# A retention layer with a Strassen-Winograd MLP: transposes in TensorE's transpose mode, another queue for k, and seven products for three quarters of block 1's first layer

## The chip, the cores and the metric

The kernel runs on one core of one Trainium2 chip. A time is the device time of one execution in microseconds (us). The median of nine executions stands for the kernel; the profile shows one execution more closely. TensorE does the matrix products, ScalarE (ACT), VectorE (DVE) and GpSimd (POOL) the elementwise work, and DMAs are issued by the queues of SyncE (SP), ACT and POOL. TensorE writes to PSUM, from where ScalarE and VectorE take its results.

## What is computed

Two stages. The first is a recurrent retention over 4 batches, 8 heads, 768 positions and 64 dimensions; the second is an MLP over the 3072 tokens that come out, 512 to 2048 to 512 wide, with a sigmoid-approximated GELU between its two layers.

```python
for t in range(S):
    state = gamma[None, :, None, None] * state + np.einsum('bhd,bhe->bhde', k[:, :, t], v[:, :, t])
    y[:, :, t] = scale * np.einsum('bhd,bhde->bhe', q[:, :, t], state)
x = y.transpose(0, 2, 1, 3).reshape(B * S, H * D)
h = x @ w_in
g = h * (1.0 / (1.0 + np.exp(-1.702 * h)))
out = g @ w_out
```

All data of q, k, v and of the result are 32-bit floats. The two weight matrices arrive as 64-bit floats and are narrowed to 32 bits on the chip.

## The kernel before

**Tiling.** The 768 positions are cut into chunks of 64, and two batches are worked on at a time, so there are 24 steps of attention, each with all 8 heads of two batches. Four steps give the 512 tokens of one block, and there are six blocks m = 0 to 5. The MLP of a block has an `up` half (x times w_in, then GELU into the tiles G) and a `down` half (G times w_out). Attention steps 0 to 7, the narrowing of both weight matrices, the `up` half of block 0 (`up0`) and the `up` half of block 1 (`up1`) come first, in an order that is written out by hand in one long string of names; after it, a loop over the blocks interleaves `down` of block m with the attention of later blocks. Blocks 2 to 5 have their `up` half (`up`, line 464 ff.) as seven products in place of eight, after Strassen and Winograd; blocks 0 and 1 have it as plain products.

**Order.** TensorE follows the program order. On the other engines, an instruction passed to `pin` (or `tc.keep_in_program_order`) keeps its place among the pinned ones of its engine; the others are placed by the framework's scheduler. Each engine works through its own queue in order, and a wait at its head holds up what is behind it. A named buffer (a tag of a pool with so many `bufs`) is given to its next user only when the last reader of the one before is done.

**The first 104 us.** For a step j below 6, `load` fetches q, k and v in their natural layout, 128 KB for each of the two batches (line 138), k of step 0 by ACT's queue and all others by SP's. `turn` (lines 239 to 249) turns q and k on TensorE, by ordinary products with a unit matrix: for every pair of heads s and s + 4 one product of 64 columns for the lower and one for the upper half of the output's partitions. The compiled program has two weight loads and two matmul instructions for every 32-bit product, so a turn of q and k together has 32 instructions. `turned` copies the result out of PSUM on ACT (line 260), `decay` scales k head by head on ACT (line 271), `attend` does the products of a step (lines 288 to 311), `masked`, `by_state`, `output`, `updated` follow on VectorE, `aged` on ACT. From step 6 on, q and k are fetched in 128-byte rows (line 155), turned by VectorE (line 252), and scaled by GpSimd (lines 273 and 358).

**Narrowing.** A weight tile of 512 KB is fetched as raw 64-bit words by SP's queue (`fetch`, line 178) into one of three raw buffers that rotate; the pair of tiles of number n uses raw buffer n modulo 3, so it waits until tile n - 3 is done. `abs` on ACT (line 205) starts the conversion, `half` (lines 209 to 211) and `rest` (lines 215 to 220) on VectorE end it. Numbers 0 to 7 are w_in, 8 to 15 w_out. A product `up0.th.p` needs w_in's number p.

**Block 1's first layer.** `up1(f)`, lines 419 to 427, for the 16 tiles f of 128 hidden units: four products of 512 columns into one PSUM tile, then `gate` (line 392) from PSUM to G on ACT. The two PSUM tiles rotate. X1, the input of block 1, lies in a part of W2 and is complete with `x7`.

**Down of block 0.** The first part of `down(0)` (line 708) needs w_out's numbers 0 and 1 in its first quarter, 2 and 3 in its second, 4 and 5 in its third, 6 and 7 (narrowing numbers 14 and 15) in its fourth. VectorE's `sums_w2` and `sums_g` (lines 446 to 457) prepare the operands of the third and later parts.

Below, "T0" is the moment when TensorE ends `up0.1.7` and goes on to block 1's first layer, 104.3 us in the profile.

Of the kernel before, what the change touches and what calls it, by code (L numbers as in the profile page):

```python
# [9 lines left out]
F32 = mybir.dt.float32  # L10
U32 = mybir.dt.uint32
AF = mybir.ActivationFunctionType
# [16 lines left out]
def kernel(  # L29
# [95 lines left out]
    def load(j, what="qkv"):  # L125

        b, c = j // NC * 2, j % NC
        rows = slice(c * D, (c + 1) * D)  # L130
        keep = tc.keep_in_program_order if j < 2 * CB else lambda i: i

        def plain(name, src, tag, bufs, engine=sp):
            t = two.tile([P, H, D], F32, name=name + "_in", tag=tag, bufs=bufs)
            QKV[name, j] = t
            for i in range(2):
                if j < NEW:
                    keep(engine.dma_start(t[i * D:(i + 1) * D], src[b + i, :, rows, :].rearrange("h p d -> p h d")))
                else:
                    for r in range(2):  # L140
                        keep(engine.dma_start(t[r * D:(r + 1) * D, i * HP:(i + 1) * HP],
                                              src[b + i, r * HP:(r + 1) * HP, rows, :].rearrange("h p d -> p h d")))

        if j < NEW:
            if "q" in what:
                plain("q", q, "q_sq", 2)
            if "k" in what:
                plain("kn", k, "k_sq", 2, sp if j else act)
        elif "q" in what:
            for name, src in (("q", q), ("k", k)):  # L150
# [88 lines left out]
    def turn(j):  # L239

        QT[j], KT[j] = home(j, "qT"), home(j, "kT")
        if j < NEW:

            x = QKV.pop(("q", j)), QKV["kn", j]
            TURNED[j] = p = [ps.tile([P, HP, P], F32, name="pt", tag="y") for i in range(2)]
            for n in (1, 0) if j else (0, 1):
                for s in range(HP):
                    for r in range(2):
                        pe.matmul(p[n][HALF[r], s, :], x[n][:, HP * r + s, :], ident, start=True, stop=True)  # L249
# [12 lines left out]
    def decay(j):  # L262

        if j % NC == NC - 1:
            return
        KD[j] = home(j, "kd")
        x = QKV["kn", j]
        if j < NEW:

            for h in range(H):  # L270
                pin(act.activation(KD[j][:, h], x[:, h], AF.Copy, scale=cold[:, H + h:H + h + 1]))
        else:
            pool.tensor_mul(KD[j].rearrange("p (i s) d -> p i s d", i=2), x.rearrange("p (i s) d -> p i s d", i=2),
                            cold[:, None, H:H + HP, None].to_broadcast([P, 2, HP, D]))
# [144 lines left out]
    def up1(f):  # L419
# [6 lines left out]
            pe.matmul(h, w, X1[:, c // 2:4:2, c % 2, :], start=(c == 0), stop=(c == 3))  # L426
        return G[:, p, ab:4:2, :], h


    def sums_w1(p):  # L430
        t, q1 = w1(p)
# [358 lines left out]

    def halves_anew():

        pool.dma_start(whole_h, bass.AP(tensor=col_decay.tensor, offset=col_decay.offset + (D - 1) * W + H,
                                        ap=[[0, P], [1, H]]))
# [16 lines left out]
    for j in range(2 * CB):  # L811
        for name in "qkv":
            works[f"{name}{j}"] = lambda j=j, name=name: load(j, name)
        works |= {f"{name}{j}": lambda j=j, do=do: do(j) for name, do in (
            ("turn", turn), ("turned", turned), ("decay", decay), ("masked", masked), ("state", by_state),
            ("x", output), ("aged", aged), ("updated", updated))}
        for f in (None, *range(2 * CB)):
            works[f"step{j}" + ("" if f is None else f"-{f}")] = lambda j=j, f=f: attend(j, f)
        works[f"step-{j}"] = lambda j=j: attend(None, j)
    for i in range(2 * NFF):  # L820
        works[f"w{i // 2}{'ab'[i % 2]}"] = lambda i=i: fetch(i)
    for name, i in [("0a", 0), ("0b", 1)] + [(str(p), 2 * p) for p in range(1, NFF)]:
# [19 lines left out]

    begin()
    for name in """
        k0 table q0 warm turn0 w0b rows warm k1 abs0b q1 turned0 step0 v0 w0a half0b mask turn1 causal rest0b
        masked0 decay0 v1 decay1 abs0a half0a step-0 updated0 turned1 q2 step1 rowd k2 whole w2b turn2 w2a x0 k3
        aged1 masked1 turned2 v2 rest0a abs2 q3 step-1 updated1 state1 decay2 aged2 step2 q4 x1 half2 decay3 w3b
        w3a up0.0.0 masked2 turn3 k4 step-2 v3 q5 rest2 k5 gate0.0.0 turned3 updated2 state2 step3 up0.0.2
        masked3 abs3 half3 x2 rest3 turn4 w1b step-3 aged3 gate0.0.2 turned4 state3 w1a w5b updated3 v5 decay4
        abs1 x3 turn5 half1 up0.0.3 turned5 up0.1.2 step4 aged4 w5a rest1 v4 gate0.0.3 decay5 w6a masked4  # L850
        gate0.1.2 abs5 w6b step5-4 half5 rest5 up0.0.1 updated4 abs6 state4 gate0.0.1 w4b
# [104 lines left out]
```

## Time and profile before

| | us |
|---|---|
| median of 9 executions | 667.01 (665.6 to 669.49) |
| the profiled execution's own time | 667.08 |
| its span, first to last instruction | 665.4 |
| granted TensorE clock, mean share | 0.997 |
| TensorE busy with matmuls | 649.7 (98%) |
| VectorE, ACT, GpSimd busy | 435.4, 148.6, 175.7 |
| `up1` of block 1 (line 426), 128 matmul instructions, on the chain of waits | 54.93 |
| turns of q and k on TensorE (line 249), 192 matmul instructions, busy | 15.8 |

The profile of one execution is read through several views. The page's first parts give the busy time of each engine and its share in 40 slices. The chain of waits follows the work that ended last back from the last instruction, at each step to what released it, in order of time: start, length, and the engine, tile and line. The timeline lists instructions of an engine by start and length, with the idle time before them and what ended it. "PE" is a matmul, "PEld" a weight load, and "SPq" an issue of a DMA by SP's queue. A busy matmul engine isn't a fast one: the busy time of pipelined matmuls overlaps and hides short gaps. So the time of a run of matmuls is best taken from the chain, where it is the distance from start to start.

### The profile page before, as it was taken

Reading aid. Unit: us, or ns where it says so; the run is one execution under the profiler, and the core shown is the slowest. Engines: PE = TensorE matmul, PEld = TensorE weight load, DVE = VectorE, ACT = ScalarE, POOL = GpSimd, SP = SyncE. Lnnn points to the kernel's source line nnn. Section 1 sums busy time; section 2 is a strip of 40 time slices with the busy share of each in tenths; the row PEclk is TensorE's granted clock in tenths of the full one; section 3 lists DMA queues with packets and bytes.
Section 4 is the critical chain, followed back from the end, with each engine's and each line's share of the span. In section 5 each row is a group of like instructions: output and inputs, shape, how many; then the busy total and the mean of one; then the engine's idle time right before and its main releaser. Section 6 shows DMA issues by size and latency. Waiting matters only on the chain.

```text
span 665.4 us, 15234 instructions
## 1 busy us (share of the span) xinstructions
PE 649.7 (98%) x6438; PEld 563.8 (85%) x6438; DVE 435.4 (65%) x618; ACT 148.6 (22%) x285; POOL 175.7 (26%) x196
## 2 busy tenths in 40 slices
PE   7899999999999999999999999999999999999997
PEld 4787875446888888888999888999888999988997
DVE  3798778788545775456985345995254995254965
ACT  5673222231000000233110234010233110233110
POOL 3000310000268326100446500345700255500000
PEclk9899999999999999999999999999999999999999
DMA  9996647442203546263385742286652253602142
GB/s 189 214 227 188 169 81 232 162 91 35 46 10 135 171 106 186 63 217 133 85 221 132 243 101 95 80 194 156 193 158 96 63 150 109 229 25 95 52 157 95
DMA packets 150500, 89.49 MB, mean 135 GB/s; under 512 B 136192, under 2 KB 137472, under 8 KB 149408
## 3 DMA queue, kind: packets, MB, share of 16 engines
q1 hardware_dynamic: 140944, 46.50, 30.5%
q0 software_dynamic: 7184, 40.78, 17.0%
q10 hardware_dynamic: 2304, 1.25, 0.7%
q8 instruction: 50, 0.82, 0.5%
q14 instruction: 18, 0.15, 0.1%
HBM read 72.89 MB, written 15.47 MB: 133 GB/s over the span
## 4 chain that ended last, share of the span: by engine, by line
PE 88%; DMA 5%; DVE 3%; SPq 2%; POOL 1%; issue 1%; ACT 0%; POOLq 0%; DVEq 0%
PE pq L575 24%; PE px L471 16%; PE pd L708 13%; PE py L471 12%; PE ph L426 8%; PE ph L413 5%; PE pa L288 2%; PE pa L296 2%; PE py L305 2%; PE py L311 2%; DMA kn_in<-in_k_dram 1%; PE pt L249 1%; DMA W<-in_moe_w_out_dram 1%; DMA k_sq<-in_k_dram 1%; DMA q_in<-in_q_dram 1%
## 5 line engine op out<-in xcount | busy, mean ns | idle before, releaser
L575 PE MATMUL pq<-W,G 128*128 128x128 f32 x672 | 80.5, 276 | 0.4 <-issue 0.4
L575 PEld LDWEIGHTS pq<-W,G 128*128 128x128 f32 x672 | 77.6, 192 | 1.2 <-issue 0.6
L544 POOL DMA_DIRECT2D ring<-W2D x28 | 15.4, 551 | 228.7 <-PE px L471 118.2
L471 PE MATMUL px<-X,W1A 128*128 128x256 f32 x256 | 60.0, 380 | 0.4 <-POOL X L441 0.4
L471 PE MATMUL px<-X,W1B 128*128 128x256 f32 x256 | 59.8, 379 | 0.0
L575 PE MATMUL pq<-ring,own 128*128 128x128 f32 x448 | 59.8, 276 | 0.0
L575 PEld LDWEIGHTS pq<-ring,own 128*128 128x128 f32 x448 | 54.5, 192 | 0.4
L471 PEld LDWEIGHTS px<-X,W1A 128*128 128x128 f32 x256 | 48.2, 190 | 7.3 <-POOL X L441 1.0
L471 PEld LDWEIGHTS px<-X,W1B 128*128 128x128 f32 x256 | 48.5, 190 | 6.7
L708 PE MATMUL pd<-W,G 128*128 128x256 f32 x224 | 49.6, 381 | 0.0
L708 PEld LDWEIGHTS pd<-W,G 128*128 128x128 f32 x224 | 42.2, 190 | 5.9
L471 PE MATMUL py<-X,W1A 128*128 128x256 f32 x192 | 45.4, 379 | 0.0
L471 PE MATMUL py<-X,W1B 128*128 128x256 f32 x192 | 45.4, 379 | 0.0
L392 ACT ACTIVATE G<-G 128x512 f32<-128x512 f32 x48 | 30.2, 630 | 52.0 <-DVE G L481 33.4
L471 PEld LDWEIGHTS py<-X,W1A 128*128 128x128 f32 x192 | 36.5, 190 | 5.0
L471 PEld LDWEIGHTS py<-X,W1B 128*128 128x128 f32 x192 | 36.5, 190 | 5.0
L489 DVE TENSOR_TENSOR t<-py,u 128x512 f32<-128x512 f32 x16 | 11.1, 692 | 32.7 <-PE py L471 32.7
L478 ACT ACTIVATE p<-px 128x512 f32<-128x512 f32 x16 | 9.6, 597 | 94.6 <-PE px L471 94.6
L575 PE MATMUL pq<-ring,G 128*128 128x128 f32 x224 | 29.6, 275 | 0.0
L575 PE MATMUL pq<-W,own 128*128 128x128 f32 x224 | 29.6, 275 | 0.0
L413 PE MATMUL ph<-X,W1A 128*128 128x256 f32 x128 | 29.0, 382 | 0.2 <-DVE X L346 0.2
L503 DVE TENSOR_TENSOR G<-G 128x512 f32<-128x512 f32 (+2 forms) x24 | 12.3, 514 | 25.7 <-ACT G L392 25.7
(206 smaller groups left out, 1165.2 us busy)
## 6 DMA issues: line engine op xcount, KB each, us to landing
ring<-W2D POOLq DMA_DIRECT2D x28, 768.0 KB, 4.8
W1B<-W1D POOLq DMA_DIRECT2D x6, 1792.0 KB, 9.4
W<-in_moe_w_in_dram SPq DMA_DIRECT2D x12, 512.0 KB, 5.7
W<-in_moe_w_out_dram SPq DMA_DIRECT2D x10, 512.0 KB, 6.1
out_dram<-o POOLq DMA_DIRECT2D x20, 256.0 KB, 3.4
q_sq<-in_q_dram SPq DMA_DIRECT2D x144, 32.0 KB, 2.3
k_sq<-in_k_dram SPq DMA_DIRECT2D x144, 32.0 KB, 2.2
v_in<-in_v_dram SPq DMA_DIRECT2D x72, 64.0 KB, 2.9
```

Of the source, the lines that this page charges most:

```text
L288: pe.matmul(pa[HALF[w], u, 0, s, :], kt[HALF[u], w, s, :], qt[HALF[u], w, s, :], start=True, stop=True)
L296: pe.matmul(pa[HALF[u], w, 1, s, :], kd[HALF[w], HP * u + s, :], vn[HALF[w], HP * u + s, :], start=True, stop=True)
L305: pe.matmul(py[HALF[o], u, 1, 2 * w + s2, :], old[HALF[u], w, 2 * s2 + o, :], qt[HALF[u], w, 2 * s2 + o, :], start=True, stop=True)
L311: pe.matmul(py[HALF[o], w, 0, 2 * u + s2 if f < NEW else 2 * s2 + u, :], vn[HALF[w], HP * u + s, :], a[HALF[w], u, s, :], start=True, stop ...
L392: pin(act.activation(g, h[:, i], AF.Gelu_apprx_sigmoid))
L413: pe.matmul(h[:, ab], w, X[:, 2 * th + c // 2, c % 2, :], start=(ab == 0 and c == 0), stop=(c == 3), skip_group_check=True)
L426: pe.matmul(h, w, X1[:, c // 2:4:2, c % 2, :], start=(c == 0), stop=(c == 3))
L471: pe.matmul(acc[:, u, :], t[:, q1 + u, sa, c, :], X[:, sb, c, :], start=(start and u == 0 and c == 0), stop=(stop and c == 1), skip_group_ ...
L503: dve.tensor_sub(q[0][1], q[0][0], q[0][1])
L544: pool.dma_start(c, W2D[i])
L575: pe.matmul(p0[:, j, :], a[:, d], w[:, d], start=(new and j == 0 and d == 0), stop=(d == NP // 2 - 1), skip_group_check=True)
L708: pe.matmul(p0[:, n, :], g1(m, p, sa)[:, n * P:(n + 1) * P], W2[:, sb, p, :], start=(new and p == 0 and n == 0), stop=(last and p == NP - ...
```

## The change

1. **Turns.** For steps 0 to 5, `turn` has, for each of q and k, four transposes of 128 columns in TensorE's transpose mode in place of eight ordinary products of 64 columns. A 128-column operand must hold heads s and s + 4 side by side, so `load` puts head n * 4 + s at place 2 * s + n. For this, each fetch of q and k of 128 KB becomes two of 64 KB. `decay` reads k at the new places.
2. **Queues and buffers of k.** From step 1 on, k goes by GpSimd's queue and not SP's. The k of steps 2 and 3 goes to the buffers of the outputs ("o"), which nothing else uses at this time, and `k2` stands before `turn1` in the order. Around it, `q2`, `updated0`, `decay1`, `masked1` and `decay3` change their places. A small fetch of GpSimd's in `halves_anew` is pinned.
3. **Seven products.** Twelve of block 1's sixteen `up1` are replaced: for d = 2, 0, 1, `seven(d, k)` has seven products of two by two tiles with 256 columns, in the scheme of `up`. GpSimd makes the sums of the operands, four for x (`seven_x`) and four for each d (`seven_w`), in buffers that the attention and the outputs use at other times. ACT copies three partial results out of PSUM for each d, VectorE adds four, and ACT gates four. `up1.12` to `up1.15` stay as they are. The narrowing of w_out (numbers 11, 10, 12, 14, 13, 15) is spread anew between them.

The diff, cut to its core:

```diff
@@ load @@
                 if j < NEW:
-                    keep(engine.dma_start(t[i * D:(i + 1) * D], src[b + i, :, rows, :].rearrange("h p d -> p h d")))
+                    to, at = t[i * D:(i + 1) * D], src[b + i, :, rows, :].rearrange("h p d -> p h d")
+                    for n in range(1 if name == "v" else 2):
+                        keep(engine.dma_start(*((to, at) if name == "v" else (to[:, n:H:2], at[:, n * HP:(n + 1) * HP]))))
...
-                plain("kn", k, "k_sq", 2, sp if j else act)
+                plain("kn", k, "k_sq" if j in (0, 1, 4, 5) else "o", 2, pool if j else act)
@@ turn @@
                 for s in range(HP):
-                    for r in range(2):
-                        pe.matmul(p[n][HALF[r], s, :], x[n][:, HP * r + s, :], ident, start=True, stop=True)
+                    pe.matmul(p[n][:, s, :], x[n][:, 2 * s:2 * s + 2].rearrange("p r d -> p (r d)"), ident, is_transpose=True)
@@ decay @@
-                pin(act.activation(KD[j][:, h], x[:, h], AF.Copy, scale=cold[:, H + h:H + h + 1]))
+                pin(act.activation(KD[j][:, h], x[:, h % HP * 2 + h // HP], AF.Copy, scale=cold[:, H + h:H + h + 1]))
@@ new, beside up1 @@
+    def seven_x():
+        for n, (tag, bufs) in ((4, ("q_sq", 2)), (5, ("k_sq", 2)), (6, ("kn", 1)), (2, ("tmp", 1))):
+            SUM_X[n] = two.tile([P, 2, TH], F32, name=f"x{n}", tag=tag, bufs=bufs)
+        for to, a, b in ((SUM_X[4], X1[:, 2], X1[:, 0]), (SUM_X[5], X1[:, 3], SUM_X[4]),
+                         (SUM_X[6], X1[:, 3], X1[:, 2]), (SUM_X[2], X1[:, 1], SUM_X[5])):
+            pin(pool.tensor_sub(to, a, b))
+    def seven_w(d):
...
+        pin(pool.tensor_add(m[4], w[2], w[3]))
+        pin(pool.tensor_sub(m[5], m[4], w[0]))
+        pin(pool.tensor_sub(m[6], w[0], w[2]))
+        pin(pool.tensor_sub(m[2], w[1], m[5]))
+    def seven(d, k):
...
+        acc = SEVEN[f"y{k}" if k in (1, 3, 5) else "x"]
+        product(acc, (0, 1, 5, 4, 6, 2, 3)[k], (0, 1, 5, 4, 6, 3, 2)[k], k in (0, 1, 3, 5), k in (1, 3, 5, 6))
+        if k == 0:
+            kept("p1", "s1", acc)
+        elif k == 1:
+            pin(dve.tensor_add(a[0], acc, SEVEN["p1"]))
+            hidden(a[0], a[0])
+        elif k == 2:
+            kept("u", "s2", acc)
+        elif k == 3:
...
+            pin(dve.tensor_add(SEVEN["t"], acc, SEVEN["u"]))
+        elif k == 4:
+            kept("vv", "s3", acc)
+        elif k == 5:
+            pin(dve.tensor_add(a[3], SEVEN["y3"], SEVEN["vv"]))
+            hidden(a[3], a[3])
+            pin(dve.tensor_add(a[2], acc, SEVEN["t"]))
+            hidden(a[2], a[2])
+        else:
+            hidden(a[1], acc)
@@ the order @@
-        k0 table q0 warm turn0 w0b rows warm k1 abs0b q1 turned0 step0 v0 w0a half0b mask turn1 causal rest0b
-        masked0 decay0 v1 decay1 abs0a half0a step-0 updated0 turned1 q2 step1 rowd k2 whole w2b turn2 w2a x0 k3
-        aged1 masked1 turned2 v2 rest0a abs2 q3 step-1 updated1 state1 decay2 aged2 step2 q4 x1 half2 decay3 w3b
-        w3a up0.0.0 masked2 turn3 k4 step-2 v3 q5 rest2 k5 gate0.0.0 turned3 updated2 state2 step3 up0.0.2
+        k0 table q0 warm turn0 w0b rows warm k1 abs0b q1 turned0 step0 v0 w0a half0b mask k2 turn1 causal rest0b
+        masked0 decay0 q2 v1 step-0 updated0 turned1 decay1 step1 rowd masked1 abs0a half0a whole w2b turn2 w2a x0 k3
+        aged1 turned2 v2 rest0a abs2 q3 step-1 updated1 state1 decay2 aged2 step2 q4 x1 half2 w3b
+        w3a up0.0.0 masked2 turn3 k4 step-2 v3 q5 rest2 k5 turned3 gate0.0.0 decay3 updated2 state2 step3 up0.0.2
...
-        w11a w11b step-7 state7 x7 half9 w10b w10a up0.1.7 rest9 gate0.1.7 abs11 half11 up1.8 gate1.8
-        w12a w12b rest11 up1.5 gate1.5 up1.4 gate1.4 abs10 half10 up1.0 gate1.0 rest10 up1.3 gate1.3 abs12
-        aged7 updated7 up1.2 gate1.2 w14b w14a half12 up1.6 gate1.6 rest12 up1.9 gate1.9 abs14 half14 w13a w13b
-        up1.11 gate1.11 rest14 up1.10 gate1.10 abs13 half13 w15a w15b up1.7 gate1.7 rest13 abs15 half15 up1.12
-        gate1.12 late_loads up1.13 gate1.13 rest15 up1.15 gate1.15 up1.14 gate1.14 up1.1 gate1.1
+        w11a w11b step-7 state7 x7 half9 w10b w10a seven_w2 up0.1.7 rest9 gate0.1.7 abs11
+        seven_x seven2.0 seven2.1 half11 seven2.2 seven2.3 w12a w12b rest11 seven2.4 seven2.5 aged7 seven_w0 abs10 seven2.6
+        seven0.0 seven0.1 half10 seven0.2 seven0.3 rest10 w14b w14a seven0.4 seven0.5 seven_w1 abs12 seven0.6
+        updated7 seven1.0 seven1.1 half12 seven1.2 seven1.3 rest12 w13a w13b seven1.4 abs14 seven1.5 half14
+        seven1.6 up1.12 rest14 gate1.12 abs13 half13 w15a w15b late_loads up1.13 gate1.13 rest13 abs15 half15
+        up1.15 gate1.15 rest15 up1.14 gate1.14
```

More of the change, by code (lines that the diff above doesn't have):

```diff
@@ L427, in up1 @@
         return G[:, p, ab:4:2, :], h
+    SUM_X, SUM_W = {}, {}
+    def seven_x():
[5 more added lines that the diff above has]
+    def seven_w(d):
+        t, q1 = w1(2 * d)
+        w = [t[:, q1:q1 + 2, s].rearrange("p u c f -> p u (c f)") for s in range(4)]
+        SUM_W[d] = {4: one.tile([P, 2, 2 * P], F32, name="w4", tag="qT", bufs=2),
+                    5: one.tile([P, 2, 2 * P], F32, name="w5", tag="at", bufs=2),
+                    6: two.tile([P, 2, 2 * P], F32, name="w6", tag="o"),
+                    2: one.tile([P, 2, 2 * P], F32, name="w2", tag="kT")}
+        m = SUM_W[d]
+        pin(pool.tensor_add(m[4], w[2], w[3]))
+        pin(pool.tensor_sub(m[5], m[4], w[0]))
+        pin(pool.tensor_sub(m[6], w[0], w[2]))
+        pin(pool.tensor_sub(m[2], w[1], m[5]))
@@ new lines, with product, kept @@
+    SEVEN = {}
+    def seven(d, k):
+        t, q1 = w1(2 * d)
+        a = [G[:, 2 * d:2 * d + 2, s, :] for s in range(4)]
+        def product(acc, sa, sb, start, stop):
+            for u in range(2):
+                for c in range(2):
+                    w = SUM_W[d][sa][:, u, c * P:(c + 1) * P] if sa in (4, 5, 6, 2) else t[:, q1 + u, sa, c, :]
+                    x = SUM_X[sb][:, c, :] if sb in SUM_X else X1[:, sb, c, :]
+                    pe.matmul(acc[:, u, :], w, x, start=(start and u == 0 and c == 0), stop=(stop and c == 1),
+                              skip_group_check=True)
+        def kept(name, tag, src):
+            SEVEN[name] = one.tile([P, 2, TH], F32, name=name, tag=tag)
+            pin(act.activation(SEVEN[name], src, AF.Copy))
+        if k in (0, 1, 3, 5):
+            SEVEN["x" if k == 0 else f"y{k}"] = ps.tile([P, 2, TH], F32, name="ph", tag="x" if k == 0 else "y")
+        acc = SEVEN[f"y{k}" if k in (1, 3, 5) else "x"]
[8 more added lines that the diff above has]
+        elif k == 3:
+            SEVEN["t"] = one.tile([P, 2, TH], F32, name="t", tag="s1")
+            pin(dve.tensor_add(SEVEN["t"], acc, SEVEN["u"]))
[8 more added lines that the diff above has]
+            hidden(a[1], acc)
@@ L791, in halves_anew @@
     def halves_anew():
-        pool.dma_start(whole_h, bass.AP(tensor=col_decay.tensor, offset=col_decay.offset + (D - 1) * W + H,
-                                        ap=[[0, P], [1, H]]))
+        pin(pool.dma_start(whole_h, bass.AP(tensor=col_decay.tensor, offset=col_decay.offset + (D - 1) * W + H,
+                                            ap=[[0, P], [1, H]])))
         pool.tensor_copy(mask[HALF[1], 0], mask[HALF[1], 1])
@@ L819 @@
         works[f"step-{j}"] = lambda j=j: attend(None, j)
+    works["seven_x"] = seven_x
+    for d in range(NP // 2):
+        works[f"seven_w{d}"] = lambda d=d: seven_w(d)
+        for n in range(7):
+            works[f"seven{d}.{n}"] = lambda d=d, n=n: seven(d, n)
     for i in range(2 * NFF):
```

## The prediction

> **What bounds the kernel now.** I read the page's busy times and slices first, then the chain of waits in order of time, then the timeline of each queue where the chain leaves TensorE.
>
> ```profile
> PE 649.7 (98%) x6438; PEld 563.8 (85%) x6438; DVE 435.4 (65%) x618; ACT 148.6 (22%) x285; POOL 175.7 (26%) x196
> ...
> DMA  9996647442203546263385742286652253602142
> ```
>
> TensorE is the bound, and only work taken from it, or a wait of it, can shorten the run. The DMA row shows where this may fail: the first 50 us (three slices of 16.6 us) have the DMA engines busy for 90% or more.
>
> ```profile
> 19.89 3.01 PE pt L249 x32
> ...
> 38.09 1.90 PE pt L249 x32
> ...
> 90.42 2.10 DMA k_sq<-in_k_dram
> ...
> 104.45 54.93 PE ph L426 x128
> ...
> 266.23 1.73 PE px L471 x8
> ```
>
> In this chain (start, length) a turn costs 1.90 us. The one at 19.89 had waited 1.47 us for k of step 2, by TensorE's timeline, and took 3.01 at a lower clock. `up1` runs unbroken: 54.93/128 = 0.429 us per instruction. A product of the seven costs 1.73 us for eight instructions, 0.216 each.
>
> The timeline shows three limits beside TensorE: SP's queue, the narrowing of weights 3 (ACT, then VectorE, then the `up0.0.3` that reads it), and VectorE held by GpSimd:
>
> ```profile
> 20.20 6.09 SPq L138 DMA_DIRECT2D q_in<-in_q_dram  x4
> ...
> 26.39 1.15 SPq L178 DMA_DIRECT2D W<-in_moe_w_in_dram  x2
> ...
> 34.92 1.15 ACT L205 ACTIVATE W1A<-W 128x1024 f32<-128x1024 f32 x1 [2.12 <-DMA W<-in_moe_w_in_dram]
> ...
> 41.29 1.23 DVE L220 TENSOR_TENSOR W1A<-W 128x1024 f32<-128x1024 f32 x1
> ...
> 43.38 7.17 PE L413 MATMUL ph<-X,W1A 128*128 128x256 f32 x32
> ...
> 178.08 1.57 POOL L461 TENSOR_TENSOR W1A<-W1A 128x512 f32<-128x512 f32 x1 [2.18 <-DVE W1A L457]
> ...
> 178.56 1.64 DVE L456 TENSOR_TENSOR W1A<-W1A 128x512 f32<-128x512 f32 x1
> ```
>
> Weights 3 are ready at 41.29 + 1.23 = 42.5, and TensorE reads them at 43.38: 0.9 us of slack. The last line takes 1.64 us; the same form takes 0.69 with GpSimd at rest.
>
> **What the Trainium skill says.** "TensorE: Matmul & The Clock Gate", Terms, calls the transpose mode 4 times faster for 32-bit data; its Part 4 gives about 275 to 390 ns for a transpose of 16-bit data. No transpose by TensorE's mode is in this trace, so these are bounds. "SBUF — State Buffer", Who interferes with whom: a VectorE operation with two inputs in SBUF and a GpSimd one that reads SBUF exclude each other, one with at most one such input doesn't. The trace agrees: 1.64 against 0.69 us above, while line 346 (PSUM and SBUF) keeps 0.69 beside GpSimd. "DMA: Bandwidth & Descriptors", Issuing engines are not separate DMA queues: another queue saves only issue time. The trace shows 0.60 to 0.64 us for such an issue on SP, and longer where it waits.
>
> **Part 1, the turns.** An ordinary 128-column product is two instructions of 0.112 us (the chain has 6.25 us for 56 at line 575), 0.223. A quarter is 0.056: eight make 0.45 us a turn. At the skill's 0.275 to 0.39 they make 2.2 to 3.1 us, a loss of up to 1.2 a turn. I take 0.1 us each, 0.8 a turn, nearer to the page on 32-bit data: 1.1 us saved, six times, 6.6 us of TensorE. The copies on ACT and the scaling by heads keep their forms and cost nothing new. Splitting q's fetches adds two SP issues a step, 1.3 us; in step 0 they postpone q's landing (6.05 us now) by perhaps 0.5, which the faster first turn covers.
>
> **Part 2, the queues.** k2 no longer waits for step 0's scaling (12.8 us) to free its buffer, so the 1.47 us wait at 19.89 goes. TensorE could then reach `up0.0.3` about 1.5 + 6.6 = 8.1 us earlier, at 35.3. It will wait there for weights 3. Their fetches were issued at 26.4 because q4 waited on SP for q2's turn (20.2 to 26.3). With six issues of k less and ten of q more SP has rather more to issue ahead of them, but q2 is turned earlier: 32 issues of 0.64 us, with q4 behind a turn 2 that ends near 17.5, come to 21.6. The DMA engines had room for this: their busy share in 22 to 28 us is 0.67, 0.40 and 0.86, some 2.1 us lost. Against it, k4 and k5 leave GpSimd's queue as soon as they can and go in between: four transfers of 128 KB, landing 0.66 us apart under load, 2.6 us. So weights 3 land between 4 us earlier and 0.5 later; I take 3. What the five k cost GpSimd, 20 issues of about 0.75 us (its longest issues today), is hidden: it is idle there but for the mask at 12 us.
>
> Weights 3 are then ready at 39.5, and `up0.0.3` starts at 39.6, 3.8 us earlier. From there VectorE is full: three operations of step 3 (1.8 us), weights 1 (5.9), then `masked4` at 47.5, which TensorE reaches at 39.6 + 7.8 = 47.4. Afterwards everything hangs on the chain weights 5, SP's fetches of q6 to v6 (17 us), weights 7 and 9, q7, k7 (landing 92.5), step 7. It moves as a whole. A little is lost on ACT's order; I put the gain at T0 at **3.3 us**, from -0.5 to 6. So half of part 1's TensorE time turns into waits for weights 3.
>
> **Part 3, the seven products.** Twelve `up1` are 12 x 4 x 2 x 0.429 = 41.2 us; 21 products of 1.73 are 36.3. TensorE saves **4.9 us**. Added: VectorE 12 additions out of PSUM (0.62 apart), 7.4 us; ACT 9 more 128x512 passes, 5.4 us, in 39 us of idle time of this stage; GpSimd 16 sums of 1.27 us, 20.3 us, on an idle engine. VectorE is the tight one: of the 55 us it is busy 46.6.
>
> I walked the queues in the written order from T0: `half` 2.7, `rest` 3.2, ACT 0.55 to 1.05, PSUM readers 0.3 us behind TensorE, a fetch landing 4.8 us after issue, GpSimd and two-input VectorE operations excluding each other. For the kernel before, the walk ends `up1` at 54.9 and `rest15` at 48.1 (trace: 54.9, 47.9). For the new order:
> - `seven2.2` adds to the PSUM tile that ACT must first have copied, and this copy stands behind `abs11`, which waits for weights 11. If they land as now, 4.8 us after T0 (ACT waits for them until 109.24), TensorE stalls 3.05 us. But now SP issues k8 and v8 ahead of them, at 97.5 to 103.4; k8 cannot go early any more, its buffer holds a sum. So their issue follows `rest8` (T0 - 3.5) and lands about T0 + 2: stall 0.25 us.
> - `p1` of d = 0 stands behind `abs10` and VectorE's additions, held by GpSimd: 1.15 us.
> - `gate1.12` waits for `rest14`, so `abs13` comes at 44.4, and VectorE ends `rest15` at 57.3. The last quarter of down's first part waits 0.8 us for it and ends at 59.1, against 61.8 before.
> So 2.7 us arrive, not 4.9. Then VectorE has 11.9 us of sums and turns ahead of `sums_g`, which may begin 11.1 us after `rest15` by TensorE's clock and is just in time today (0.3 us wait at 186.7): I count 0.8 lost, up to 3. Net **1.9 us**, from -3 to 4.5. The late fetches of q8 to k9 end near T0 + 53, before their turn; no cost. From block 2 on nothing changes.
>
> **Sum.** 3.3 + 1.9 = 5.2 us. The profiled execution has 667.08 us, 1.7 of it outside the span, and the median is 667.01, so 667.0 - 5.2 = **661.8**.
>
> **Rivals.**
> - **The front gives nothing** (0.2): k4, k5 and the split fetches keep weights 3 at 34.8, or the transposes cost as much as the products. The DMA row speaks for it, the dip at 22 to 28 us against. Gain 0.8 + 1.9: 664.3.
> - **Both gains arrive** (0.2): weights 3 land 4 us earlier and ACT's order costs nothing (6), VectorE is nowhere late (4): 657.
> - **VectorE becomes the bound of block 1, slower** (0.12). Sixteen GpSimd sums, each holding VectorE for 0.95 us (1.64 - 0.69), are 15.2 us, where my walk finds the additions and idle gaps absorbing nearly all. `rest15` then ends near T0 + 68, down's first part at 70, 8 us later than before; less 3.3 from the front: 672. It decides once `rest15` passes T0 + 63.3 (61.8 - 1.8 + 3.3). For it: VectorE is 85% full here; against: the sums are early and needed late, and PSUM additions aren't held.
> - The likeliest case, part of each: 0.48, 659.5 to 664.
>
> **Chances and range.** A measurement of this kernel tells about 0.2%, 1.3 us, from no change. Likeliest, second rival and most of the first (0.15) are faster: 0.83. Same 0.06 (the rest of the first and a mild third). Slower 0.11. The range, 657.5 to 666.3, leaves out the fastest part of the second rival and most of the third.
>
> **What would show it.** Turns: line 249's group with 48 or 96 matmuls, a turn near 0.8 us in the chain or less; over 1.9 refutes it. Queues: no wait for k of step 2, TensorE waiting instead for weights 3 ahead of `up0.0.3`, near 39.6; weights 3 fetched near 21.6. T0 near 101. Seven: 168 matmuls of 0.216 us in place of 96 of 0.429, `abs11` early, `rest15` near T0 + 57, two-input VectorE operations of 1.6 us and more. I am wrong if TensorE waits for VectorE through block 1, or if T0 hasn't moved.

## The result and the profile after

The changed kernel takes **671.27 us** (median of 17 runs, 669.36 to 674.85), the kernel before 667.45 beside it (54 runs): a ratio of 1.0056, 95% interval 1.0044 to 1.0069. It is slower by 3.8 us, where 5.2 us less were forecast. The profiled execution has 672.84 us, its span 671.1 (665.4 before). Line numbers below are those of the kernel after, and in the experiments those of each run's own kernel; they differ from those of the printed kernel.

The page of the kernel after, the engines' busy times and the DMA row of its 40 slices:

```profile
PE 645.6 (96%) x6366; PEld 575.2 (86%) x6366; DVE 449.8 (67%) x630; ACT 153.1 (23%) x294; POOL 215.2 (32%) x232
...
DMA  9995544325314446445287662277562143512142
```

TensorE has 72 matmul instructions fewer (144 less for turns, 72 more for products) and is busy 4.1 us less, yet the span is 5.7 us longer: TensorE waits. GpSimd is busy 39.5 us more: 20 issues for k of 0.63 us each, and sums that take 1.7 us each in the mean where 1.27 were reckoned.

The chain of waits, in order of time (start, length, what):

```profile
14.54 1.90 PE pt L250 x8
...
22.93 9.62 DMA q_in<-in_q_dram
32.68 0.64 PE pt L250 x4
...
42.67 0.87 PE pt L250 x8
...
108.62 2.20 POOL w L452
110.82 1.68 POOL x L439
112.57 2.13 POOL x L439
114.75 35.31 PE ph L467 x152
150.06 13.73 PE ph L427 x32
```

A turn has eight instructions instead of 32. The one at 42.67 costs 0.87 us (1.90 before); the one at 14.54, with 1.90, has waits in it. But the chain now runs over the fetch of q of step 3, and later over GpSimd, which hands the products their sums of x at 114.7, ten microseconds behind T0. The timeline shows both places. The front first:

```profile
20.57 9.71 SPq L140 DMA_DIRECT2D q_in<-in_q_dram  x8
...
30.37 1.06 SPq L180 DMA_DIRECT2D W<-in_moe_w_in_dram  x2
...
32.68 0.63 PE L250 MATMUL pt<-ident,q_in 128*128 128x128 f32 x4 [2.65 <-DMA q_in<-in_q_dram]
...
37.17 5.50 PE L414 MATMUL ph<-X,W1A 128*128 128x256 f32 x16
...
43.62 1.24 DVE L222 TENSOR_TENSOR W1A<-W 128x1024 f32<-128x1024 f32 x1
...
45.97 7.07 PE L414 MATMUL ph<-X,W1A 128*128 128x256 f32 x32
```

Weights 3 are fetched at 30.4 (26.4 before, 21.6 in the forecast), behind eight issues of q. TensorE waits 2.65 us for q of step 3, then works at a lower clock for a while (5.50 us for a block that takes 3.72; the granted clock was 0.67 in this stretch), and starts `up0.0.3` at 45.97 instead of 43.38. T0 is 104.7 (104.3 before). A single T0 says little, though: the eight profiled executions with this front as it is (all but `early_sums` and `front_w3`) have 101.9 to 104.7, the five with before's front 103.4 to 107.3. What the front is worth has to come from the medians below. Then the products:

```profile
104.70 3.62 PE L467 MATMUL ph<-W,W1B 128*128 128x256 f32 x16
...
105.86 1.64 DVE L212 TENSOR_SCALAR W<-W 128x1024 uint32<-128x1024 uint32 x1
107.02 1.60 POOL L451 TENSOR_TENSOR w<-w,W1A 128x512 f32<-128x512 f32 x1
107.53 2.17 DVE L213 SCALAR_TENSOR_TENSOR W<-W 128x1024 uint32<-128x1024 uint32 x1
...
108.58 2.24 POOL L452 TENSOR_TENSOR w<-W1A 128x512 f32<-128x512 f32 x1
...
110.78 1.71 POOL L439 TENSOR_TENSOR x<-W 128x512 f32<-128x512 f32 x1
...
112.57 2.12 POOL L439 TENSOR_TENSOR x<-W,x 128x512 f32<-128x512 f32 x1
...
114.75 1.65 PE L467 MATMUL ph<-x,w 128*128 128x256 f32 x3 [6.43 <-POOL x L439]
```

TensorE stands 6.43 us. Three sums of weights (`w`, lines 450 to 452) stand ahead of the sums of x although `seven_x` comes first in the written order: the state's decay between them (line 359) isn't pinned, so it moved ahead, and the pinned `seven_w0` written behind it came with it. So an unpinned operation between two pinned ones let them change places here, which the description of `pin` above leaves out. And VectorE and GpSimd hold each other up: line 212's operation, 0.69 us by itself, takes 1.64, line 213's 2.17 instead of 1.23, a sum up to 2.25.

**The balance** of this one execution, against before's: T0 0.4 later; `up` ends at T0 + 59.1 instead of 55.1, 4.0; from there to the end of the waits for VectorE's sums of w_out and g it takes 29.4 us instead of 27.4, 2.0 (these waits are 0.9 and 1.2 us, 0.3 before); 0.7 comes back later: 5.7. The medians differ by 3.8.

### The profile page after: what moved, and what is told of

Read it like the earlier page. It is cut to its first block, busy times and chain, and to the rows that moved or that the text cites. A ratio compares the mean times of both kernels' runs of the same rounds, so it can differ in the third digit from the quotient of the medians.

```text
span 671.1 us, 15199 instructions
## 1 busy us (share of the span) xinstructions
PE 645.6 (96%) x6366; PEld 575.2 (86%) x6366; DVE 449.8 (67%) x630; ACT 153.1 (23%) x294; POOL 215.2 (32%) x232
## 3 DMA queue, kind: packets, MB, share of 16 engines
q1 hardware_dynamic: 135856, 45.19, 29.4%
## 4 chain that ended last, share of the span: by engine, by line
PE 84%; DMA 6%; POOL 4%; DVE 3%; SPq 2%; issue 1%; ACT 0%; POOLq 0%; DVEq 0%; ACTq 0%
PE pq L643 24%; PE px L539 16%; PE pd L776 13%; PE py L539 12%; PE ph L467 5%; PE ph L414 4%; PE ph L427 2%; PE pa L289 2%; DMA q_in<-in_q_dram 1%; PE py L312 1%; PE pa L297 1%; DMA kn_in<-in_k_dram 1%; PE py L306 1%; DMA W<-in_moe_w_out_dram 1%; DMA k_sq<-in_k_dram 1%
## 5 line engine op out<-in xcount | busy, mean ns | idle before, releaser
L393 ACT ACTIVATE G<-G 128x512 f32<-128x512 f32 x57 | 35.7, 630 | 67.7 <-DVE G L549 33.4
L414 PE MATMUL ph<-X,W1A 128*128 128x256 f32 x128 | 30.7, 398 | 0.5 <-DVE X L347 0.5
```

The source lines that it names most:

```text
L393: pin(act.activation(g, h[:, i], AF.Gelu_apprx_sigmoid))
L414: pe.matmul(h[:, ab], w, X[:, 2 * th + c // 2, c % 2, :], start=(ab == 0 and c == 0), stop=(c == 3), skip_group_check=True)
```

## The experiments

Each ratio is against the kernel before on the same chip, with its 95% interval. The recorded texts number the theories anew: in the first group theory 1 says that the front is held by what lands and that the products lose by GpSimd's order; from the second group on it is the exclusion of VectorE and GpSimd.

### The two halves

`front_only`: the change with before's order from T0 on.

```diff
-        ... w10b w10a seven_w2 up0.1.7 rest9 gate0.1.7 abs11 seven_x seven2.0 ...
+        ... w10b w10a up0.1.7 rest9 gate0.1.7 abs11 half11 up1.8 gate1.8 ...
```

> The change without its seven products: turns, queues and buffers of k as in the change, block 1's first layer as before. Theory 1 (k on GpSimd's queue delays q3 and weights 3 on SP's queue and eats what the turns save; the rest of the loss is in block 1): 667.5, T0 near 104.7, as in the change. Rival (the front gains and the whole loss, larger than it looks, is in block 1): 663 to 664.

667.25, ratio 0.9992 [0.9975, 1.0009], T0 104.6. The front gains nothing that can be told: 0.25% (1.7 us) at most by the interval, where 3.3 us were forecast.

`seven_only`: before's fetches, turns and front order, with the seven products.

```diff
-                    for n in range(1 if name == "v" else 2):
-                        keep(engine.dma_start(*((to, at) if name == "v" else (to[:, n:H:2], ...))))
+                    keep(engine.dma_start(t[i * D:(i + 1) * D], src[b + i, :, rows, :].rearrange("h p d -> p h d")))
...
-                plain("kn", k, "k_sq" if j in (0, 1, 4, 5) else "o", 2, pool if j else act)
+                plain("kn", k, "k_sq", 2, sp if j else act)
...
```

> The seven products alone, with the turns and the queues of the kernel before. Theory 1 (GpSimd makes the sums of the next weights ahead of the sums of x, TensorE waits 6.4 us for them and runs on at half clock): slower by 5 us, 672. Rival (the seven products gain by themselves and lose only together with the new front): 664 or less.

673.64, 1.008 [1.0058, 1.0103]; TensorE waits 6.53 us for GpSimd at 114.65, as in the whole change. So the loss is the products'.

### The order on GpSimd, and the sums

`aged7_pinned`: the whole change, the decay kept in its place.

```diff
-            pool.tensor_mul(new..., old..., whole_h...)
+            i = pool.tensor_mul(new..., old..., whole_h...)
+            if f == NEW + 1:
+                pin(i)
```

> The whole change, with GpSimd's scaling of the state of step 7 pinned in its place, so that GpSimd makes the four sums of x ahead of it and of the sums of the next weights. Theory 1 (the order on GpSimd's queue is the cause): the wait of 6.4 us and the slow clock behind it go, 664, up-stage near 51.5 us. Rival (VectorE and GpSimd exclude each other so much that the sums or the narrowing come late in any order): 669 to 671.

672.41, 1.0068 [1.0036, 1.0101]: that theory fell, and the rival's 669 to 671 is nearer. The sums of x are ready at 108.6 and the wait of 6.43 us is gone, but other waits took its place. TensorE's waits from 100 to 165 us (in all, times, longest):

```profile
PE ph L469 <- DVE G L493: 3.7, 1, 3.7
PE ph L469 <- ACT u L474: 3.1, 1, 3.1
PE ph L469 <- ACT p L474: 2.1, 2, 1.3
```

From here on, the decay is pinned in every run that has the change's products.

`no_sums`: the sums left out; the products read plain operands, so this kernel doesn't compute the layer.

```diff
-        pin(pool.tensor_add(m[4], w[2], w[3]))
...
-                    w = SUM_W[d][sa][...] if sa in (4, 5, 6, 2) else t[:, q1 + u, sa, c, :]
+                    w = t[:, q1 + u, sa % 4, c, :]
```

> The whole change (GpSimd's decay of the state kept in its place) without GpSimd's sixteen sums of the seven products: the products read plain operands of the same sizes instead, so what they compute is not the up-projection. TensorE's listed instructions, ACT's copies, VectorE's additions and the order of the work stay. Theory 1 (GpSimd's sums and VectorE's narrowing exclude each other operation by operation, and that sum bounds the stage): the narrowing takes 0.69 and 1.23 us again, the last of it ends by T0+58, the up-projections end by T0+53, and the time is 662.5 to 665.5. Rival A (the chain of TensorE, ACT's copy, VectorE's addition and the gate behind it is what is slow, whoever makes the sums): 669 or more. Between: each holds a part.

666.16, 0.9969 [0.9954, 0.9984]. Without the sums 6.6 us go (1.0068 less 0.9969); even then only 2.1 of the 5.2 us forecast arrive: between theory 1 and rival A. The profiled execution waited 2.87 us for `p`, behind `abs11`, which could take up weights 11 only at T0 + 4.8.

`early_sums`: seven sums of weights ahead of T0.

```diff
-        ... gate0.1.3 aged6 step7-6 masked7 ...
+        ... gate0.1.3 aged6 seven_wa2 seven_wb2 step7-6 masked7 seven_wa0 ...
...
```

> The whole change with the decay of the state kept in its place, and seven of GpSimd's sums of the weights (four of the third double product, three of the first) made some 15 us earlier, where VectorE has gaps. Theory 1 (exclusion bounds the stage behind T0): seven operations times 0.94 us leave that stage, of which VectorE's gaps ahead of it hold about 7 us, so 666 to 669 instead of 672.4. Rival A (chain of additions): no change, 671 to 673. Rival B (the gaps are not there, the sums hold up the last narrowings ahead of T0): 672 or more, with T0 later than 102.

671.22, 1.0047 [1.0029, 1.0066]. As rival B says, T0 came late: 107.0 (101.9 in `aged7_pinned`'s execution), while the stage behind it shrank to 55. The time itself is just under rival B's 672.

`no_sums_w11` and `sums_w11`: `abs11` behind the third product, without and with the sums.

```diff
-        ... gate0.1.7 abs11 seven_x seven2.0 seven2.1 half11 seven2.2 seven2.3 ...
+        ... gate0.1.7 seven_x seven2.0 seven2.1 seven2.2 abs11 seven2.3 half11 ...
```

> As the whole change without GpSimd's sums (plain operands of the same sizes in their place, so the up-projection is not what is computed), with one more edit: the step on ACT that takes weights 11 up is listed behind the third product instead of ahead of the first. Theory 3 (without the sums, what eats the products' 4.9 us is that weights 11 land 4.6 us behind T0, ACT takes its instructions in order, and the copy of the first product stands behind them: 2.87 us of wait and 1.5 us of half clock after it): both go, the up-projections end at T0+50 to T0+51.5, and the time is 661 to 663. Rival (VectorE then is late with weights 11's own narrowing or with the first addition): 665 to 667.

> The whole change with the decay of the state in its place, and weights 11 on ACT behind the third product; GpSimd makes its sums. Theory 1 (with the sums, the exclusion of VectorE and GpSimd bounds the stage): little of the 4.4 us arrives, 669.5 to 672. Rival (the order on ACT was the larger loss in the whole change too): 666 to 668.

665.45, 0.9975 [0.996, 0.999], and 671.86, 1.0067 [1.0042, 1.0093]. In the first, `up` ends at T0 + 52.3 in the profiled execution (55.0 in `no_sums`), yet the ratios don't differ: theory 3 isn't borne out, and how often the 2.87 us wait occurs stays open. Both pairs put the sums under the products at 6 us and more.

### Do the sums cost by themselves?

`sums_added`: before, with the sixteen sums, used by nothing.

```diff
-        ... w10b w10a up0.1.7 rest9 gate0.1.7 abs11 half11 up1.8 ...
+        ... w10b w10a seven_w2 up0.1.7 rest9 gate0.1.7 abs11 seven_x half11 up1.8 ...
...
```

> The kernel before with GpSimd's sixteen sums of the seven products added at their places and used by nothing: the up-projections are the sixteen ordinary ones. Theory 1 (each sum takes 0.94 us from VectorE, and VectorE's sum then is the bound): the narrowing of weights 15 ends 15 us later than before's T0+48, at T0+63, about where TensorE needs it, so 667.5 to 670. Theory 4 (the delay of VectorE reaches TensorE only through the seven products' additions, which TensorE waits for at once): TensorE's waits up to T0+55 stay as before, 667 to 668.5. Rival (the sums cost 6 us wherever they stand): 672 to 674.

669.29, 1.0022 [1.0008, 1.0036]. In the profiled execution T0 came late (107.3), but from T0 to the end of `up` it took 55.1 us as before. Busy time in stretches of it (PE, PEld, DVE, ACT, POOL, each with its instructions, then PEclk, the granted TensorE clock, the DMA share and GB/s):

```profile
107.00:121.00 14.00, 14.00 (x35) 6.31 (x34) 13.79 (x8) 4.58 (x7) 13.92 (x9) 1.00 0.56 189
121.00:135.00 14.00, 14.00 (x34) 6.27 (x33) 13.76 (x9) 3.47 (x6) 11.48 (x6) 1.00 0.47 144
```

GpSimd and VectorE are both busy nearly all the time, holding each other up, and behind T0 TensorE doesn't notice; weights 15 are ready at T0 + 55.0, 7 us later than before, in time. So "each sum costs its microsecond" fell too. What differs under the products is who waits for VectorE and GpSimd.

`two_late`: two double blocks only, behind four ordinary products, before's front.

```diff
+        up0.1.7 rest9 gate0.1.7 abs11 half11 up1.8 gate1.8 w12a w12b rest11 seven_x up1.9 gate1.9 up1.10 gate1.10
+        abs10 half10 up1.11 gate1.11 rest10 aged7 seven_w0 abs12 updated7 seven0.0 seven0.1 w14b w14a half12 seven0.2 seven0.3
...
```

> Seven products for two of the four double blocks, and late: the front, its queues and turns are those of before; behind T0 four ordinary up-projections come first, then seven products for the first and the second double block, so that GpSimd has 12 sums instead of 16 and they run where VectorE has 14 us to spare. Theory 1 (a price of 0.94 us of VectorE for each sum, felt only where VectorE ends last): two double blocks save 3.3 us of TensorE, the sums over GpSimd's outputs are 0.5, so 664.5 to 666. Rival (any sum of GpSimd in this stage costs its 0.94 us at the end): 667.5 + 11.3 - 3.3 is 675, with half of it hidden 669 to 671.

675.15, 1.0129 [1.0094, 1.0163]: worse than the change, with fewer sums. Its timeline shows why in one place:

```profile
119.03 0.60 ACT L473 ACTIVATE p<-ph 128x512 f32<-128x512 f32 x1
...
130.81 0.68 DVE L482 TENSOR_TENSOR G<-ph,p 128x512 f32<-128x512 f32 x1
...
131.52 0.63 ACT L394 ACTIVATE G<-G 128x512 f32<-128x512 f32 x1 [11.90 <-DVE G L482]
132.06 0.58 ACT L473 ACTIVATE u<-ph 128x512 f32<-128x512 f32 x1
...
132.78 1.62 PE L468 MATMUL ph<-x,w 128*128 128x256 f32 x3 [8.62 <-ACT u L473]
```

VectorE makes the first addition at 130.8, because ten microseconds of narrowing and a state update stand ahead of it in its queue; ACT's gate waits for the addition, the copy `u` behind the gate waits with it, and TensorE, which is to add to that PSUM tile, waits 8.62 us until `u` is out.

`gates_late`: as `sums_w11`, the gate behind the copy.

```diff
             pin(dve.tensor_add(a[0], acc, SEVEN["p1"]))
-            hidden(a[0], a[0])
         elif k == 2:
             kept("u", "s2", acc)
+            hidden(a[0], a[0])
```

> The whole change with the state's decay in its place and weights 11 later on ACT, as before, and with ACT's gate of the first addition of each double block listed behind the copy of the third product. Theory 4 (TensorE's wait of 4.9 us for that copy comes from VectorE's addition by way of the gate ahead of the copy): the copy comes 3 to 5 us sooner for the first double block; VectorE is no faster, so the next addition is waited for instead: 669 to 671.5. Rival (ACT's order is what the products lost by): 666 to 668.

675.03, 1.011 [1.008, 1.0139]. The wait for `u` (4.9 in `sums_w11`) is gone, and 7.1 and 1.9 us are waited for VectorE's additions instead. Theory 4 named this exchange of waits, but not its size: it had 669 to 671.5, and the run is slower than `sums_w11`.

`adds_first`: `two_late` with VectorE's additions ahead of the narrowing and the gates behind the copies.

```diff
-        abs10 half10 up1.11 gate1.11 rest10 aged7 seven_w0 abs12 updated7 seven0.0 seven0.1 w14b w14a half12 seven0.2 seven0.3
+        abs10 up1.11 gate1.11 aged7 seven_w0 seven0.0 seven0.1 half10 seven0.2 seven0.3 seven0.4 seven0.5 rest10 abs12 w14b w14a
...
```

> As the run with seven products for two double blocks behind four ordinary up-projections and the front of before, with the order on VectorE and ACT changed: VectorE's additions stand ahead of the narrowing they stood behind, and ACT's gates of these sums behind the next copy out of PSUM. Theory 4 (the sums hurt only through additions and gates queued behind the narrowing): the waits of 8.6 and 1.3 us and the half clock after them go, TensorE saves 3.3 us listed and loses up to 1.5 at the later sums: 664 to 666.5. Rival (VectorE and GpSimd together are too long for the stage, so the wait comes back at another addition or at weights 15): 669 or more.

**665.2, 0.9958 [0.9942, 0.9973]**: 1.7% less than `two_late` by the ratios, some 11 us, with the same sums on the same engines. TensorE's instructions come in the same order in both; the edit moves those of VectorE and ACT. (GpSimd's order differs in one pair of neighbours and SP's in some fetches, both only from 131 us on, when most of the long wait is over.) It is faster than the kernel before by 0.4%, and than the change. The same stretch:

```profile
122.49 0.60 ACT L473 ACTIVATE u<-ph 128x512 f32<-128x512 f32 x1 [2.86 <-PE ph L468]
123.30 0.68 DVE L482 TENSOR_TENSOR G<-ph,p 128x512 f32<-128x512 f32 x1
...
125.74 1.89 PE L468 MATMUL ph<-W,w 128*128 128x256 f32 x8
```

`u` is out 9.6 us sooner; TensorE waits for none of these results, and `up` ends at T0 + 51.8, 3.3 us less than before.

`adds_first_front`: the same with the change's front.

> The same with the change's front (transposes, split fetches, k on GpSimd's queue, its order). Theory 2 (this front gains and loses nothing against the one of before): as the run with the front of before, within 1.5 us, 664 to 666.5. Rival (it gives back 3 us, as predicted for it): 661 to 663.

665.26, 0.9965 [0.9946, 0.9984]: the front again adds nothing. This order for all three double blocks of the change was not run, so whether the whole change can gain by it is open.

### The front taken apart

`turns_only`: before with transposes and the split fetches, queues and order as before. `split_only`: before with nothing but the split, which is the edit shown.

```diff
-                    keep(engine.dma_start(t[i * D:(i + 1) * D], src[b + i, :, rows, :]...))
+                    for n in (slice(0, H),) if name == "v" else (slice(0, HP), slice(HP, H)):
+                        keep(engine.dma_start(to[:, n], at[:, n]))
```

> The turns in transpose mode alone, with the split fetches, everything on SP's queue and in the order of the kernel before. Theory 1 (GpSimd's queue eats the gain): faster, 664, TensorE's turns 0.9 us each. Rival (weights 3 hold TensorE whatever the queue): 666.5 to 667.5.

> The kernel before with nothing but its fetches of q and k of steps 0 to 5 split in two halves of the heads, all on the queues they had. Theory 2: the same loss as with the transposes, or more, as no turn gets shorter: 672.5 to 675, T0 at 109 to 111. Rival C (splitting costs nothing, and the 6 us of the turns alone came from the transposes): 667 to 668.5, T0 at 104 to 105.

673.39, 1.0074 [1.0052, 1.0095], and 674.51, 1.01 [1.0076, 1.0124]. No theory had the first; theory 2 had the second. The split by itself costs 6.7 us. The transposes win back some 1.7 of it, which isn't clear of the noise (the intervals overlap). Stretches of `split_only` and of before, the last two columns DMA share and GB/s:

```profile
0.00:10.00 10.00, 5.18 (x26) 2.94 (x28) 0.17 (x2) 1.76 (x3) 3.12 (x10) 1.00 0.69 139
10.00:20.00 10.00, 6.88 (x144) 4.64 (x140) 5.59 (x10) 6.41 (x22) 2.79 (x4) 1.00 0.77 154
```

```profile
0.00:10.00 10.00, 5.60 (x34) 3.68 (x34) 1.37 (x5) 2.64 (x4) 3.12 (x10) 1.00 0.92 165
10.00:20.00 10.00, 6.97 (x170) 4.71 (x168) 7.66 (x13) 7.17 (x23) 2.79 (x4) 1.00 1.22 252
```

With twice the issues at some 0.64 us each, SP's queue starts less data than the DMA engines moved before (a share of 0.77 against 1.22 from 10 to 20 us). Taking k off this queue, with its new buffers and the new order (`front_only` against `turns_only`), gives 0.8% back; the balance is the zero of `front_only`.

`queues_only`: `front_only` with whole fetches and ordinary turns. `k_turned_alone`: `front_only` with only k split and transposed; its edit, without the turn's:

```diff
-                    for n in range(1 if name == "v" else 2):
+                    for n in range(2 if name == "kn" else 1):
...
```

> The first half of the change without its transposes: k of steps 1 to 5 by GpSimd's queue and into the outputs' buffers, with the new order, but q and k fetched whole and turned by ordinary products as before. Theory 2 (each fetch split in two costs SP's queue its 0.6 us per further issue, and that is where the front's gain went; the queue for k is what would have gained): T0 at 102 to 103.5 and 664.5 to 666.5. Rival C (neither the split nor the issues matter at the end, weights 3 are bound by the data that moves): T0 at 104 to 105 and 667 to 668. Rival D (the turns' 0.9 us each do count): 668 to 671.

> The first half of the change with only k split and turned by transposes, on GpSimd's queue; q is fetched whole on SP's queue and turned by ordinary products. Theory 2 (SP's issues, 0.62 us each, pace the front: the split alone cost 6.6 us, and k on the other queue won it back): SP has 12 issues fewer in the first 35 us than with both split, so weights 3 come 3 us sooner, T0 at 101.5 to 103.5 and 664.5 to 666.5. Rival C (VectorE, busy over 9 of 10 us from 30 to 60 us, bounds the front whatever lands): T0 at 104 to 105 and 667 to 668. Rival E (it goes as with k on GpSimd's queue and nothing split): T0 near 110 and 673.

673.25, 1.0078 [1.005, 1.0106], and 673.43, 1.0097 [1.0067, 1.0127]. No theory had the first, and only rival E's number fits the second. TensorE's timeline of `k_turned_alone`:

```profile
33.83 0.46 PE L293 MATMUL pa<-G 64*64 64x64 f32 x16 [0.28 <-DVE state L372]
38.45 0.70 PE L293 MATMUL pa<-G 64*64 64x64 f32 x16 [4.16 <-issue]
39.08 5.72 PE L418 MATMUL ph<-X,W1A 128*128 128x256 f32 x16
```

TensorE stops for 4.16 us in the middle of a step, waiting for no semaphore. Such stops come after the 449th, 961st and 1217th instruction of TensorE in this execution (2.07, 4.16 and 0.51 us; matmuls, weight loads and semaphore waits counted), and after the 705th and 1473rd in `queues_only` (2.89 and 0.53 us): always 193 and a multiple of 256. The queue of instructions brings 16 KB at a time (50 packets in the kernel after, for 12,857 such instructions: one for 257), and this place's packet ran from 35.4 to 37.0, within the stop. So TensorE had run out of instructions, and they came late, in a stretch with a DMA share of 1.18. The stops add up to 6.7 us in `k_turned_alone`, whose T0 is 5.6 later than before's, and to 3.4 in `queues_only`, 6.3 later. That makes them a likely part of the loss, but doesn't show it: `seven_only` has two of 1.85 and 1.04 us and a T0 only 0.2 later, and no run took them away. `turns_only` and `split_only` have none in their first 100 us, so the loss by the split is another one. Why moving k alone costs 0.8% stays open.

`front_w3`: `front_only` with the fetch of weights 3 ahead of q of step 4.

```diff
-        ... step2 q4 x1 half2 w3b w3a up0.0.0 ...
+        ... step2 x1 half2 w3b w3a q4 up0.0.0 ...
```

> The first half of the change alone (transposes, split fetches, k on GpSimd's queue, the new order), with the fetch of weights 3 listed on SP's queue ahead of q of step 4 instead of behind its four issues. Theory 2 (the front's gain hangs on when weights 3 land: VectorE stands 2.85 us for them, then TensorE 0.94): the fetch is issued near 25.5 us instead of 29.7, lands near 33, TensorE's fourth up-projection starts 2 to 3 us sooner, T0 at 101.8 to 103, 664.5 to 666. Rival C (what lands sooner is waited for elsewhere: q of step 4, or weights 4 and on): T0 at 104 to 105, 667 to 668.

668.05, 1.0003 [0.9984, 1.0022], T0 104.6: rival C. The fetch is issued at 26.6, three microseconds sooner, `up0.0.3` starts 0.8 sooner, and 0.2 is left one block later.

## Why the prediction was wrong

- **Turns: right.** 0.8 us a turn were forecast; where a turn doesn't wait, 0.87 and 1.02 are in the chain. TensorE's busy time for turns falls from 15.8 to 9.3 us, about the 6.6 forecast. This comes of 0.1 us an instruction, a choice between two bounds.
- **Queues: wrong, and with it the 3.3 us at T0** (measured: 0.4 later). The step that failed is "32 issues of 0.64 us ... come to 21.6": weights 3 were issued at 30.4. The eight issues of q took 9.71 us, because one of them lasted 4.17 where the others took 0.61 to 1.09. The semaphore that it waits for had been complete at 21.4, before it began at 22.9; what held it is open. The kernel before has such issues too, and the prediction misread them. It took 20.2 to 26.3 for a wait of q4 on q2's turn, which an earlier turn would shorten. But the long issues there are the two of q3, 2.92 and 1.76 us; turn 2 had ended at 22.9, and q4 was issued behind them at 25.0, in 0.6 us each. The long issues, first of the kernel after, then of the kernel before:

```profile
22.93 4.17 SPq L140 DMA_DIRECT2D q_in<-in_q_dram  x1
```

```profile
20.20 2.92 SPq L138 DMA_DIRECT2D q_in<-in_q_dram  x1
...
23.16 1.76 SPq L138 DMA_DIRECT2D q_in<-in_q_dram  x1
```

In 20 to 30 us the DMA share rose from 0.83 to 1.19, so the "room" was not there. In the profiled execution weights 2 land at 27.7 (23.6 before), and TensorE waits for q of step 3. Even weights 3 ahead of q4 would not have helped (`front_w3`). From 30 to 60 us VectorE is busy 26.8 us of 30, before and after alike, which leaves little to gain; that this is the floor is argued, not shown. The first rival, "the front gives nothing", is what happened.

- **Products on TensorE: right**, as far as their own time goes. In `adds_first`, two double blocks save 3.3 us of 55.1; the forecast's prices give 27.5 less 24.2, also 3.3.
- **The walk of the queues: wrong.** It let 2.7 us arrive; the whole stage lost 4.0. Three of its terms failed. First, it took the written order for GpSimd's order: one unpinned operation put the sums of x behind three others (6.43 us of wait). Second, it made only two-input operations of VectorE exclude GpSimd. I had left out half of what the pages say: the Trainium skill, "GPSIMD Engine Reference", Key points, names VectorE's 2-port perf mode beside two SBUF inputs. The trace agrees in so far as half of the narrowing's operations have one input and go from 0.69 to 1.64 us beside GpSimd's sums; in which mode they run, it doesn't show. So six passes for each number of the weights can be held and not three, and a sum beside them takes 1.6 to 2.25 us, not 1.27. Third, it put VectorE's lateness down mainly at weights 15 and once, with 1.15 us, at `p1` of d = 0, not at each addition as it stands in the queue: with the order on GpSimd mended, 3.7 us are waited for one addition and 3.1 for the copy `u` behind another (`aged7_pinned`).
- **The third rival had the number (672) and not the mechanism.** Its point was passed (weights 15 ready at T0 + 64.7, past 63.3), but TensorE didn't wait for them, only for the later sums behind them. `sums_added` has all sixteen sums and loses 0.2%. The cost arises where a product of TensorE waits for a sum, a copy or an addition, and these stand in order behind work that nobody needs yet. `two_late` against `adds_first` shows it for two double blocks: some 11 us by the order on VectorE and ACT. For the whole change it is argued from its waits. That the rival's number came so close is luck.
- **Later sums:** 0.8 lost were forecast, 2.0 measured in the profiled execution.

## What to carry to other kernels

A replacement with fewer products also moves who waits for whom: before, only ACT stood between TensorE and its next PSUM tile; after, VectorE and GpSimd did, and VectorE's queue held ten microseconds of work due much later (`two_late`). Before pricing the engines' sums, list for each new instruction what stands ahead of it in its own queue and who waits for it, and place what TensorE needs ahead of what is only due some time. And an issue of a DMA isn't free because it is short: at 0.64 us each, twice as many for q and k were 1% of this kernel.

## What the runs showed of the hardware

- A transpose of 128x128 32-bit elements in TensorE's transpose mode is one matmul instruction here, against two for an ordinary product, and eight in a row take 0.87 us: 0.11 us each.
- TensorE's instructions come by DMA, some 256 at a time (packets of 16 KB). Stops of 2.07, 2.89 and 4.16 us in mid-step fell where such a packet landed only within the stop, in stretches with a DMA share of 1.1 to 1.3; the timeline has them only as "issue". That the packets came late because of the data is likely, not shown.
- VectorE's additions with one operand in PSUM keep 0.68 us beside a busy GpSimd, while its operations with one or two inputs in SBUF go from 0.69 to 1.64 and from 1.23 to 2.17 (128x1024 elements).
- After waits of 2.65 and 6.43 us, TensorE took 5.50 us for a block of 3.72 and 7.69 for one of 5.34; the granted clock was 0.67 from 37.17 to 42.67 us, and 0.71 from 114.75 to 122.5.
